# A new order of all engines, another split of the early copies, and a third output tile

## The chip, the cores and the metric

The kernel runs on one core of a Trainium2 chip. The metric is the device time of one execution in microseconds (us), and the time before is the median of three runs. Engines: PE (TensorE, matmuls; PEld is its weight load), DVE (VectorE), ACT (ScalarE), POOL (GpSimd) and SP (SyncE). SP and POOL mostly issue DMAs here.

## What is computed

The inputs are q, k and v of 4 batches, 8 heads, 768 positions and 64 channels, and a feed-forward layer with w_in (512 x 2048), w_out (2048 x 512) and six coefficients. All are float32 in DRAM.

```
scores = q @ k^T / 8, kept where key < 4 or 0 <= query - key < 128
x = softmax(scores) @ v                     -> rows (batch, position), 512 columns
h = x @ w_in
P = a0 + a1 h + a2 h^2 + a3 h^3
Q = 1 + |b0| |h| + |b1| h^2
out = (P / (Q + 1e-6)) @ w_out              -> 3072 x 512, float32
```

## The kernel before, in words

The 3072 output rows are cut into 12 steps of 256 rows, three to a batch. For a step PE makes `scores` (four pieces, one for each pair of heads and half), ACT takes `exps` of them, PE does `attend` (two pieces, scores times V), DVE does `rec` and `norm`, the result is turned (`turn_x`, `placed_x`), and `gemm1` (four pieces of 16 matmuls, one for each quarter of w_in) makes h. ACT copies h to SBUF (`copy_in`) and makes the logarithm and exponential of the reciprocal (`ln`, `exp`); DVE makes the polynomials (`and`, `sqd`, `den`, `even`, `odd`, `odd_h`, `num`, `gate`); PE closes with `gemm2` (four pieces), ACT copies the result out (`copy_out`) and SP stores it. PSUM has four pairs of banks, ps_h, ps_o, ps_m and ps_s, and each piece of PE takes one pair until the copy behind it has freed it.

Each of these is a named piece (`piece`, L1010 and on). The list `ORDER` (L18) gives the number of every piece in the order in which the program issues it, so each engine's queue and each DMA queue runs its pieces in just that order, and an engine that waits for one piece holds all behind it. `ENGINE` says which of ACT and DVE does an early copy, `BANK` which pair of banks a piece takes. A negative number in `ORDER` is a spin of matmuls on constant data (`spin`, L720). No planner runs in the kernel.

Inputs: q and k of step 0 come as float32 on the SP and ACT queues and are cast on chip. All else comes through POOL's one queue and is made bfloat16 on the way: `load_kc`, `load_qc` and `load_vc` (256 KB, Q of step 3 384 KB, Q of step 2 128 KB in SBUF) for K and Q of steps 1 to 3 and V of steps 0 to 2, turned on PE and placed by ACT or DVE; `load_k` and `load_q` (128 KB) for later steps, turned by a DMA transposition of SP; `load_v` (32 or 64 KB a head); `load_w_in` and `load_w_out` (four quarters of 512 KB each). `hold` (L504) is a tiny POOL copy that reads a late element of a result, so that POOL issues nothing behind it until then.

Order of POOL's loads in the opening, before: V0, Q1, K1, V1, Q3, K2, w_in 0, Q2, w_in 1, w_in 3, hold for x of step 0, a head of V3, K3, w_in 2, V2, two heads of V, K5b, K4b, two heads of V, Q tiles 9 and 10, ... The second spin stands in PE's queue ahead of `turn_vs` 1.

Of the kernel before, what the change touches and what calls it, by code (L numbers as in the profile page):

```python
# [65 lines left out]
def kernel(  # L66
# [54 lines left out]
    ENGINE = {('cast_q0', 1): 'DVE',  # L121
               ('place_kc', 3, None): 'DVE',
               ('place_qc', 0, 0): 'ACT',
               ('place_qc', 0, 1): 'ACT',
               ('k_sink', 0): 'DVE',
# [29 lines left out]
             ('attend', 1, 0): 'ps_h',
             ('attend', 1, 1): 'ps_s',
             ('attend', 2, 0): 'ps_m',
             ('attend', 2, 1): 'ps_h',
             ('attend', 3, 0): 'ps_h',
             ('attend', 3, 1): 'ps_m',  # L160
# [21 lines left out]
             ('gemm1', 1, 1): 'ps_o',
             ('gemm1', 1, 2): 'ps_o',
             ('gemm1', 1, 3): 'ps_m',
             ('gemm1', 2, 0): 'ps_m',
             ('gemm1', 2, 1): 'ps_o',
             ('gemm1', 2, 2): 'ps_m',
             ('gemm1', 2, 3): 'ps_o',
# [7 lines left out]
             ('gemm1', 4, 3): 'ps_o',
             ('gemm1', 5, 0): 'ps_s',
             ('gemm1', 5, 1): 'ps_m',
             ('gemm1', 5, 2): 'ps_o',
             ('gemm1', 5, 3): 'ps_h',  # L200
             ('gemm1', 6, 0): 'ps_m',
             ('gemm1', 6, 1): 'ps_o',
# [1227 lines left out]
```

## Time and profile before

| what | value |
|---|---|
| median of three runs | 232.0 us (231.14 to 232.74) |
| the profiled execution | 232.42 us, span 230.7 us |
| PE busy | 215.9 us (94%) |
| DVE busy | 211.1 us (91%) |
| ACT busy | 207.0 us (90%) |
| POOL busy | 97.3 us (42%) |
| moved by DMA | 26.98 MB, mean 117 GB/s; POOL's queue 65024 packets |

The span runs from the first to the last instruction; the 1.7 us between it and the time lie around it. Busy time counts each engine by itself, so three engines of over 90% leave little room: an engine's idle time is worth something only if the other two can use it too. PE's busy time has the spins in it.

### The profile page before, as it was taken

The page shows a single profiled execution, that of the slowest core. Times are in us where ns is not written, and L with a number is a line of the kernel's source. Part 1 is how long each engine was busy: PE and PEld are TensorE (multiplying, and loading weights), DVE is VectorE, ACT ScalarE, POOL GpSimd, SP SyncE. Part 2 cuts the span into 40 slices and gives each one's busy share as a digit, 9 for nine tenths or more (in the row PEclk, how much of TensorE's full clock was granted, in tenths as well). Part 3 has the DMA queues.
Part 4 walks back from the last instruction along what each step waited for, and adds up shares of the span by engine and source line. Part 5 has one row for each costly group of instructions (what it writes and reads, how often), then busy time and mean ns, then how long its engine had stood idle before and what let it go on. Part 6 is the DMA issues. An engine that isn't in the chain of part 4 may idle for free.

```text
span 230.7 us, 7350 instructions
## 1 busy us (share of the span) xinstructions
PE 215.9 (94%) x3249; PEld 147.0 (64%) x3271; DVE 211.1 (91%) x251; ACT 207.0 (90%) x177; POOL 97.3 (42%) x126
## 2 busy tenths in 40 slices
PE   8768999989999999999999999999999999999992
PEld 2546777778747667667677577758856875544441
DVE  3595699879999999999999999999999999999991
ACT  2757889989997999999999999999999999799961
POOL 8914756967559499988199800000000000000000
PEclk9999999999999999999999999999999999999999
DMA  6999999999999999999969998230050200400152
GB/s 182 199 191 199 197 144 103 135 117 121 205 176 141 130 106 150 172 122 124 196 155 133 109 148 162 47 71 0 3 139 3 48 0 0 182 4 0 49 224 91
DMA packets 95237, 26.98 MB, mean 117 GB/s; under 512 B 85862, under 2 KB 92262, under 8 KB 95206
## 3 DMA queue, kind: packets, MB, share of 16 engines
q0 software_dynamic: 65024, 12.98, 90.4%
q1 hardware_dynamic: 28942, 12.75, 29.8%
q10 hardware_dynamic: 1240, 0.79, 1.1%
q8 instruction: 25, 0.41, 0.8%
q14 instruction: 6, 0.05, 0.1%
HBM read 27.30 MB, written 6.29 MB: 146 GB/s over the span
## 4 chain that ended last, share of the span: by engine, by line
PE 69%; DMA 19%; POOL 3%; DVE 3%; issue 2%; ACT 2%; SPq 0%; DVEq 0%; ACTq 0%
PE ps_s L974 13%; PE ps_h L974 11%; PE ps_o L910 9%; PE ps_m L974 9%; PE ps_m L910 7%; DMA w_out_sb<-in_moe_w_out_dram 6%; PE ps_s L910 5%; PE ps_h L910 5%; DMA stage_v<-in_v_dram 4%; DMA k_bf<-in_k_dram 3%; DMA stage_a<-in_k_dram 2%; POOL v L465 2%; DMA ab_row<-in_moe_a_dram 2%; PE ps_o L846 2%; DMA q_bf<-in_q_dram 1%
## 5 line engine op out<-in xcount | busy, mean ns | idle before, releaser
L910 PEld LDWEIGHTS <-w_in_sb 128*128 128x128 bf16 x768 | 73.8, 98 | 13.0 <-issue 1.2
L974 PEld LDWEIGHTS <-g 128*128 128x128 bf16 x386 | 36.4, 98 | 41.6 <-issue 1.4
L954 ACT ACTIVATE lnq<-den 128x4096 f32<-128x4096 bf16 (+3 forms) x18 | 44.6, 2482 | 1.5 <-DVE den L935 1.4
L959 ACT ACTIVATE den<-lnq 128x4096 bf16<-128x4096 f32 (+3 forms) x18 | 44.5, 2484 | 0.2
L465 POOL DMA_DIRECT2D v<-in_v_dram x48 | 35.0, 746 | 3.6 <-DMA w_out_sb<-in_moe_w_out_dram 1.5
L910 PE MATMUL ps_o<-xblk,w_in_sb 128*128 128x256 bf16 x304 | 36.3, 273 | 0.0
L974 PE MATMUL ps_s<-w_out_sb,g 128*128 128x512 bf16 x136 | 32.3, 379 | 0.8 <-issue 0.5
L974 PE MATMUL ps_h<-w_out_sb,g 128*128 128x512 bf16 x121 | 28.6, 379 | 0.9 <-issue 0.5
L964 DVE TENSOR_TENSOR g<-num,den 128x4096 bf16<-128x4096 bf16 (+3 forms) x18 | 28.3, 1572 | 0.3
L935 DVE TENSOR_TENSOR den<-den,sq 128x4096 bf16<-128x4096 bf16 (+3 forms) x18 | 28.3, 1570 | 0.2
L951 DVE TENSOR_TENSOR num<-num,sq 128x4096 bf16<-128x4096 bf16 (+3 forms) x18 | 28.3, 1572 | 0.1
L948 DVE TENSOR_TENSOR sq<-sq,hb 128x4096 bf16<-128x4096 bf16 (+3 forms) x18 | 28.2, 1569 | 0.1
L910 PE MATMUL ps_m<-xblk,w_in_sb 128*128 128x256 bf16 x208 | 24.9, 273 | 0.5 <-DMA w_in_sb<-in_moe_w_in_dram 0.5
L974 PE MATMUL ps_m<-w_out_sb,g 128*128 128x512 bf16 x90 | 21.6, 379 | 0.6 <-issue 0.5
L917 ACT ACTIVATE hb<-ps_o 128x1024 bf16<-128x1024 f32 x19 | 19.5, 1029 | 2.1 <-PE ps_o L910 1.9
L924 ACT ACTIVATE sq<-hb 128x1024 bf16<-128x1024 bf16 (+3 forms) x15 | 20.0, 1341 | 0.1
L427 POOL DMA_DIRECT2D q_bf<-in_q_dram x15 | 16.7, 1111 | 6.0 <-DMA w_out_sb<-in_moe_w_out_dram 2.6
L910 PE MATMUL ps_s<-xblk,w_in_sb 128*128 128x256 bf16 x160 | 19.1, 273 | 0.0
L940 DVE TENSOR_SCALAR num<-sq,acoef 128x4096 bf16<-128x4096 bf16 (+3 forms) x18 | 18.3, 1023 | 0.3
L944 DVE TENSOR_SCALAR sq<-sq,acoef 128x4096 bf16<-128x4096 bf16 (+3 forms) x18 | 18.4, 1021 | 0.3
L507 POOL COPY seen<-x_n 1x1 bf16<-1x1 bf16 x8 | 9.7, 1225 | 17.4 <-DVE x_n L860 17.4
L926 DVE TENSOR_TENSOR sq<-hb 128x2048 bf16<-128x2048 bf16 (+2 forms) x13 | 16.8, 1295 | 0.1
(154 smaller groups left out, 321.5 us busy)
## 6 DMA issues: line engine op xcount, KB each, us to landing
out_dram<-o_t SPq DMA_DIRECT2D x11, 512.0 KB, 3.6
w_in_sb<-in_moe_w_in_dram POOLq DMA_DIRECT2D x4, 512.0 KB, 10.8
k_bf<-in_k_dram POOLq DMA_DIRECT2D x16, 128.0 KB, 6.6
w_out_sb<-in_moe_w_out_dram POOLq DMA_DIRECT2D x4, 512.0 KB, 11.7
q_bf<-in_q_dram POOLq DMA_DIRECT2D x15, 128.0 KB, 5.4
v<-in_v_dram POOLq DMA_DIRECT2D x24, 64.0 KB, 6.3
stage_v<-in_v_dram POOLq DMA_DIRECT2D x3, 256.0 KB, 9.6
v<-in_v_dram POOLq DMA_DIRECT2D x24, 32.0 KB, 5.7
```

Source lines behind the costliest of these rows:

```text
L465: nc.gpsimd.dma_start(out=v_fix[b % 2][half(r), g * NHF:(g + steps) * NHF, hl, 0:D], in_=v[b, h, g * TS:(g + steps) * TS, :].rearrange("(j ...
L910: nc.tensor.matmul(ps[:, n, :], lhsT=w_in_all[:, c, fc * P:(fc + 1) * P], rhs=xblk[m][:, c, :], start=(c == 0), stop=(c == NDMC - 1))
L917: nc.scalar.activation(out=hb[m][:, j * GW:(j + 1) * GW], in_=ps_h.pop((m, j)).rearrange("p n c -> p (n c)"), func=AF.Copy)
L924: nc.scalar.activation(out=sq[m][:, c], in_=hb[m][:, c], func=AF.Square)
L935: nc.vector.tensor_tensor(out=den[m][:, c], in0=den[m][:, c], in1=sq[m][:, c], op=ALU.add)
L944: nc.vector.tensor_scalar(out=sq[m][:, c], in0=sq[m][:, c], scalar1=a3, scalar2=a1, op0=ALU.mult, op1=ALU.add)
L948: nc.vector.tensor_tensor(out=sq[m][:, c], in0=sq[m][:, c], in1=hb[m][:, c], op=ALU.mult)
L951: nc.vector.tensor_tensor(out=num[m][:, c], in0=num[m][:, c], in1=sq[m][:, c], op=ALU.add)
L954: nc.scalar.activation(out=lnq_fix[:, c], in_=den[m][:, c], func=AF.Ln, scale=qsc_reg, bias=1.000001)
L959: nc.scalar.activation(out=den[m][:, c], in_=lnq_fix[:, c], func=AF.Exp, scale=-1.0)
L964: nc.vector.tensor_tensor(out=g_of[m][:, c], in0=num[m][:, c], in1=den[m][:, c], op=ALU.mult)
L974: nc.tensor.matmul(ps_out[own][:, tt, cols], lhsT=g_of[m][:, co:co + P], rhs=w_out_all[:, fc, cols], start=(fc == 0), stop=(fc == NFFC - 1 ...
```

## The change

`ORDER`, `ENGINE` and `BANK` are replaced as a whole. Nothing is computed otherwise, and each engine keeps its number of pieces but for one spin. What the new lists say, read piece by piece:

- POOL issues V0, Q1, K1, K2, V1, Q3, w_in 0, Q2, w_in 1, w_in 3, K3, w_in 2, Q tile 11, a head of V3, two heads of V4, a head of V3, Q tile 9, K5a, V2, Q tiles 10 and 12, a head of V3, K4a, and seven more heads of V. Then comes a hold for h of step 0, K4b, the hold for x of step 0, K5b, the holds for h and x of step 1, two heads of V4, the hold for x of step 3, three heads of V, and the four quarters of w_out.
- PE begins with a spin of 57 in place of 154 (14 matmuls of 512 columns and one of 128, before 13 and two), and the second spin (211: two of 512 and three of 128) is gone. `turn_vc` 2 stays ahead of the first `gemm1` of step 1. The scores of step 4 come behind three of the four `gemm1` of step 2 (before, ahead of all four). Between the first `gemm2` of step 0 and its second half now stand two pieces of scores and one of attend.
- Early copies move between ACT and DVE as the table below shows. On DVE the sink rows of V of batches 1 to 3 (`spread_vs` 1) come ahead of the first `norm`, before behind it.
- `o_sb` has three output tiles in place of two, and `copy_out` of step m waits for the store of step m - 3. The staging tile of the sink rows moves into the free part of the tile that holds q of step 0.

```
 ORDER = [
-    118, 2, 3, 0, -154, 108, 107, 129, 109, 117, 4, 119, 113, 116, 120, 121, 122, 1, 125, 143,
+    118, 2, 3, -57, 0, 108, 107, 109, 119, 113, 5, 117, 120, 121, 122, 129, 143, 144, 1, 125,
...
-    ENGINE = {('cast_q0', 1): 'DVE',
-               ('place_kc', 3, None): 'DVE',
+    ENGINE = {('cast_q0', 1): 'ACT',
+               ('place_kc', 3, None): 'ACT',
-               ('place_qc', 0, 1): 'ACT',
-               ('k_sink', 0): 'DVE',
+               ('place_qc', 0, 1): 'DVE',
+               ('k_sink', 0): 'ACT',
-               ('placed_x', 0, 0): 'ACT',
-               ('placed_x', 0, 1): 'DVE',
+               ('placed_x', 0, 0): 'DVE',
+               ('placed_x', 0, 1): 'ACT',
-               ('placed_x', 1, 1): 'DVE',
+               ('placed_x', 1, 1): 'ACT',
-               ('placed_x', 2, 1): 'DVE',
+               ('placed_x', 2, 1): 'ACT',
-               ('place_vc', 2): 'ACT',
-               ('cast_k0', 0): 'DVE',
-               ('place_k0', 0): 'DVE',
+               ('place_vc', 2): 'DVE',
+               ('cast_k0', 0): 'ACT',
+               ('place_k0', 0): 'ACT',
-               ('cast_q0', 0): 'ACT',
+               ('cast_q0', 0): 'DVE',
-               ('place_kc', 2, None): 'ACT',
-               ('place_qc', 3, 1): 'ACT',
-               ('k_sink', 1): 'ACT',
+               ('place_kc', 2, None): 'DVE',
+               ('place_qc', 3, 1): 'DVE',
+               ('k_sink', 1): 'DVE',
-               ('k_sink', 3): 'ACT'}
+               ('k_sink', 2): 'DVE',
+               ('k_sink', 3): 'DVE'}
...
-             ('turn_vc', 2): 'ps_s',
+             ('turn_vc', 2): 'ps_h',
...
-    o_sb = ctx.enter_context(tc.tile_pool(name="o_sb", bufs=2))
+    o_sb = ctx.enter_context(tc.tile_pool(name="o_sb", bufs=3))
...
-    stage_s = const_pool.tile([SR, B, D], FP32, name="stage_s")
+    stage_s = stage_b[0:SR, NQ0 * H * D:NQ0 * H * D + B * D].rearrange("p (b d) -> p b d", b=B)
...
-                      ends + [("store", m - 2, 0) if m >= 2 else None],
+                      ends + [("store", m - 3, 0) if m >= 3 else None],
...
-          [("gemm2", LAST, 1, parts(LAST) - 1), ("store", LAST - 2, 0)])
+          [("gemm2", LAST, 1, parts(LAST) - 1), ("store", LAST - 3, 0)])
```

## Rows read from the trace of the kernel before

**Rows 1.** Windows: stretch, length, busy PE, PEld, DVE, ACT, POOL, clock, DMA, GB/s.

```profile
6.70:21.70 15.00, 10.53 (x310) 7.98 (x310) 11.24 (x33) 10.22 (x14) 7.00 (x11) 1.00 1.64 188
21.70:31.00 9.30, 8.32 (x245) 6.82 (x242) 6.08 (x13) 8.37 (x11) 6.80 (x10) 1.00 1.51 193
...
36.40:67.50 31.10, 29.41 (x571) 23.31 (x569) 29.11 (x43) 30.22 (x33) 20.59 (x30) 1.00 2.05 144
...
67.50:192.00 124.50, 122.64 (x1867) 86.48 (x1885) 122.86 (x98) 121.03 (x90) 53.53 (x56) 1.00 1.25 102
```

**Rows 2.** Waits of PE: who waited for whom, us in total, times, longest.

```profile
PE ps_s L761 <- DMA qT<-q_bf: 0.7, 1, 0.7
...
PE ps_h L974 <- DMA w_out_sb<-in_moe_w_out_dram: 0.3, 1, 0.3
```

**Rows 3.** Timeline of POOL: start, length, what was issued, [idle before <-releaser].

```profile
20.52 0.18 POOL L507 COPY seen<-x_n 1x1 bf16<-1x1 bf16 x1 [7.94 <-DVE x_n L860]
...
22.25 0.77 POOL L511 DMA_DIRECT2D w_in_sb<-in_moe_w_in_dram  x1
22.99 0.91 POOL L474 DMA_DIRECT2D stage_v<-in_v_dram  x1
...
26.46 1.84 POOL L458 DMA_DIRECT2D k_bf<-in_k_dram  x2
...
30.74 0.90 POOL L427 DMA_DIRECT2D q_bf<-in_q_dram  x1 [1.19 <-DMA w_in_sb<-in_moe_w_in_dram]
33.33 0.89 POOL L427 DMA_DIRECT2D q_bf<-in_q_dram  x1 [1.68 <-DMA stage_v<-in_v_dram]
```

**Rows 4.** DMA view: what, queue, count, KB of each, us from issue to landing.

```profile
w_in_sb<-in_moe_w_in_dram POOLq DMA_DIRECT2D x2, 512.0 KB, 14.4
...
w_in_sb<-in_moe_w_in_dram POOLq DMA_DIRECT2D x1, 512.0 KB, 8.2
...
stage_v<-in_v_dram POOLq DMA_DIRECT2D x1, 256.0 KB, 9.6
...
k_bf<-in_k_dram POOLq DMA_DIRECT2D x2, 128.0 KB, 7.0
...
q_bf<-in_q_dram POOLq DMA_DIRECT2D x1, 128.0 KB, 5.5
...
kT<-k_bf SPq DMA_TRANSPOSE x16, 4.7
```

**Rows 5.** Timeline of PE: second spin, products of steps 0 and 1.

```profile
16.56 0.77 PE L728 MATMUL ps_o<-warm 128*128 128x512 bf16 x5
...
21.74 1.92 PE L910 MATMUL ps_o<-xblk,w_in_sb 128*128 128x256 bf16 x16
...
30.50 1.92 PE L910 MATMUL ps_m<-xblk,w_in_sb 128*128 128x256 bf16 x16 [0.53 <-DMA w_in_sb<-in_moe_w_in_dram]
...
36.40 1.92 PE L910 MATMUL ps_m<-xblk,w_in_sb 128*128 128x256 bf16 x16
```

**Rows 6.** Timeline of DVE in the opening: V0 placed, sink rows spread, second norm.

```profile
12.13 1.21 DVE L679 CAST v<-ps_o 128x1024 bf16<-128x1024 f32 x1
...
17.67 1.89 DVE L555 TENSOR_TENSOR v_sink<-ps_o,ind 128x512 bf16<-128x512 f32 x3
...
19.70 0.75 DVE L860 SCALAR_TENSOR_TENSOR x_n<-ps_s,ratio,rec 128x512 bf16<-128x512 f32 x1
```

**Rows 7.** Groups of DVE by form: count, busy us, mean ns.

```profile
L679 DVE COPY xblk<-ps_h 128x512 bf16<-128x512 bf16 x3 | 1.2, 416 | 0.7 <-PE ps_h L885 0.7
...
L679 DVE COPY kT<-ps_m 128x512 bf16<-128x512 bf16 x1 | 0.7, 671 | 0.0
...
L679 DVE COPY k_sink<-kT 64x16 bf16<-64x16 bf16 x4 | 0.7, 166 | 0.7 <-ACT kT L677 0.7
```

**Rows 8.** Groups of ACT by form: copy of h, copy of x.

```profile
L917 ACT ACTIVATE hb<-ps_o 128x1024 bf16<-128x1024 f32 x19 | 19.5, 1029 | 2.1 <-PE ps_o L910 1.9 <-issue 0.2
...
L677 ACT ACTIVATE xblk<-ps_o 128x512 bf16<-128x512 bf16 x1 | 0.6, 591 | 0.0
```

More of the change, by code (lines that the diff above doesn't have):

```diff
@@ L148 @@
-               ('place_qc', 3, 1): 'ACT',
-               ('k_sink', 1): 'ACT',
+               ('place_kc', 2, None): 'DVE',
+               ('place_qc', 3, 1): 'DVE',
+               ('k_sink', 1): 'DVE',
                ('placed_x', 3, 0): 'DVE',
                ('k_sink', 2): 'DVE',
-               ('k_sink', 3): 'ACT'}
-    BANK = {('attend', 0, 0): 'ps_s',
+               ('k_sink', 3): 'DVE'}
+    BANK = {('attend', 0, 0): 'ps_m',
              ('attend', 0, 1): 'ps_s',
[L155 to L160, printed above, removed]
+             ('attend', 1, 0): 'ps_m',
+             ('attend', 1, 1): 'ps_m',
+             ('attend', 2, 0): 'ps_o',
+             ('attend', 2, 1): 'ps_m',
+             ('attend', 3, 0): 'ps_s',
+             ('attend', 3, 1): 'ps_o',
@@ L161 @@
              ('attend', 4, 0): 'ps_m',
-             ('attend', 4, 1): 'ps_o',
-             ('attend', 5, 0): 'ps_m',
-             ('attend', 5, 1): 'ps_h',
+             ('attend', 4, 1): 'ps_s',
+             ('attend', 5, 0): 'ps_s',
+             ('attend', 5, 1): 'ps_m',
              ('attend', 6, 0): 'ps_m',
-             ('attend', 6, 1): 'ps_o',
+             ('attend', 6, 1): 'ps_h',
              ('attend', 7, 0): 'ps_s',
-             ('attend', 7, 1): 'ps_o',
-             ('attend', 8, 0): 'ps_s',
@@ L170 @@
-             ('attend', 8, 1): 'ps_h',
+             ('attend', 7, 1): 'ps_s',
+             ('attend', 8, 0): 'ps_m',
+             ('attend', 8, 1): 'ps_s',
              ('attend', 9, 0): 'ps_s',
              ('attend', 9, 1): 'ps_o',
-             ('attend', 10, 0): 'ps_s',
-             ('attend', 10, 1): 'ps_o',
+             ('attend', 10, 0): 'ps_h',
+             ('attend', 10, 1): 'ps_s',
              ('attend', 11, 0): 'ps_o',
-             ('attend', 11, 1): 'ps_s',
-             ('gemm1', 0, 0): 'ps_o',
@@ L178 @@
-             ('gemm1', 0, 1): 'ps_s',
-             ('gemm1', 0, 2): 'ps_m',
-             ('gemm1', 0, 3): 'ps_o',
-             ('gemm1', 1, 0): 'ps_s',
[L182 to L188, printed above, removed]
+             ('attend', 11, 1): 'ps_h',
+             ('gemm1', 0, 0): 'ps_h',
@@ L189 @@
+             ('gemm1', 0, 1): 'ps_o',
+             ('gemm1', 0, 2): 'ps_s',
+             ('gemm1', 0, 3): 'ps_m',
+             ('gemm1', 1, 0): 'ps_s',
+             ('gemm1', 1, 1): 'ps_m',
+             ('gemm1', 1, 2): 'ps_s',
+             ('gemm1', 1, 3): 'ps_o',
+             ('gemm1', 2, 0): 'ps_o',
+             ('gemm1', 2, 1): 'ps_h',
+             ('gemm1', 2, 2): 'ps_o',
+             ('gemm1', 2, 3): 'ps_s',
              ('gemm1', 3, 0): 'ps_o',
              ('gemm1', 3, 1): 'ps_m',
-             ('gemm1', 3, 2): 'ps_s',
+             ('gemm1', 3, 2): 'ps_h',
@@ L192 @@
              ('gemm1', 3, 3): 'ps_s',
-             ('gemm1', 4, 0): 'ps_o',
-             ('gemm1', 4, 1): 'ps_o',
+             ('gemm1', 4, 0): 'ps_s',
+             ('gemm1', 4, 1): 'ps_h',
              ('gemm1', 4, 2): 'ps_m',
[L196 to L202, printed above, removed]
+             ('gemm1', 4, 3): 'ps_h',
@@ L203 @@
+             ('gemm1', 5, 0): 'ps_m',
+             ('gemm1', 5, 1): 'ps_s',
+             ('gemm1', 5, 2): 'ps_m',
+             ('gemm1', 5, 3): 'ps_o',
+             ('gemm1', 6, 0): 'ps_o',
+             ('gemm1', 6, 1): 'ps_m',
              ('gemm1', 6, 2): 'ps_s',
              ('gemm1', 6, 3): 'ps_o',
-             ('gemm1', 7, 0): 'ps_m',
-             ('gemm1', 7, 1): 'ps_m',
+             ('gemm1', 7, 0): 'ps_h',
+             ('gemm1', 7, 1): 'ps_o',
              ('gemm1', 7, 2): 'ps_o',
-             ('gemm1', 7, 3): 'ps_s',
@@ L209 @@
-             ('gemm1', 8, 0): 'ps_s',
+             ('gemm1', 7, 3): 'ps_m',
+             ('gemm1', 8, 0): 'ps_m',
              ('gemm1', 8, 1): 'ps_s',
@@ L231 @@
              ('gemm2', 6, 0, 0): 'ps_m',
-             ('gemm2', 7, 0, 0): 'ps_s',
+             ('gemm2', 7, 0, 0): 'ps_o',
              ('gemm2', 8, 0, 0): 'ps_m',
-             ('gemm2', 9, 0, 0): 'ps_s',
-             ('gemm2', 10, 0, 0): 'ps_h',
-             ('gemm2', 11, 0, 0): 'ps_s',
-             ('gemm2', 11, 1, 0): 'ps_o',
-             ('scores', 0, 0): 'ps_h',
-             ('scores', 0, 1): 'ps_s',
-             ('scores', 0, 2): 'ps_s',
-             ('scores', 0, 3): 'ps_m',
-             ('scores', 1, 0): 'ps_m',
-             ('scores', 1, 1): 'ps_s',
-             ('scores', 1, 2): 'ps_m',
-             ('scores', 1, 3): 'ps_h',
-             ('scores', 2, 0): 'ps_m',
-             ('scores', 2, 1): 'ps_h',
-             ('scores', 2, 2): 'ps_o',
-             ('scores', 2, 3): 'ps_o',
-             ('scores', 3, 0): 'ps_o',
-             ('scores', 3, 1): 'ps_s',
-             ('scores', 3, 2): 'ps_o',
-             ('scores', 3, 3): 'ps_h',
-             ('scores', 4, 0): 'ps_s',
+             ('gemm2', 9, 0, 0): 'ps_h',
+             ('gemm2', 10, 0, 0): 'ps_o',
+             ('gemm2', 11, 0, 0): 'ps_h',
+             ('gemm2', 11, 1, 0): 'ps_s',
+             ('scores', 0, 0): 'ps_m',
+             ('scores', 0, 1): 'ps_m',
+             ('scores', 0, 2): 'ps_h',
+             ('scores', 0, 3): 'ps_s',
+             ('scores', 1, 0): 'ps_m',
+             ('scores', 1, 1): 'ps_h',
+             ('scores', 1, 2): 'ps_h',
+             ('scores', 1, 3): 'ps_s',
+             ('scores', 2, 0): 'ps_h',
+             ('scores', 2, 1): 'ps_o',
+             ('scores', 2, 2): 'ps_s',
+             ('scores', 2, 3): 'ps_h',
+             ('scores', 3, 0): 'ps_s',
+             ('scores', 3, 1): 'ps_m',
+             ('scores', 3, 2): 'ps_h',
+             ('scores', 3, 3): 'ps_o',
+             ('scores', 4, 0): 'ps_m',
              ('scores', 4, 1): 'ps_s',
@@ L259 @@
              ('scores', 5, 1): 'ps_o',
-             ('scores', 5, 2): 'ps_o',
-             ('scores', 5, 3): 'ps_m',
+             ('scores', 5, 2): 'ps_m',
+             ('scores', 5, 3): 'ps_o',
              ('scores', 6, 0): 'ps_m',
              ('scores', 6, 1): 'ps_o',
-             ('scores', 6, 2): 'ps_h',
+             ('scores', 6, 2): 'ps_m',
              ('scores', 6, 3): 'ps_h',
@@ L268 @@
              ('scores', 7, 2): 'ps_m',
-             ('scores', 7, 3): 'ps_h',
-             ('scores', 8, 0): 'ps_s',
-             ('scores', 8, 1): 'ps_h',
-             ('scores', 8, 2): 'ps_m',
+             ('scores', 7, 3): 'ps_o',
+             ('scores', 8, 0): 'ps_m',
+             ('scores', 8, 1): 'ps_o',
+             ('scores', 8, 2): 'ps_o',
              ('scores', 8, 3): 'ps_o',
-             ('scores', 9, 0): 'ps_s',
+             ('scores', 9, 0): 'ps_h',
              ('scores', 9, 1): 'ps_s',
-             ('scores', 9, 2): 'ps_o',
-             ('scores', 9, 3): 'ps_o',
+             ('scores', 9, 2): 'ps_h',
+             ('scores', 9, 3): 'ps_s',
              ('scores', 10, 0): 'ps_s',
              ('scores', 10, 1): 'ps_o',
-             ('scores', 10, 2): 'ps_o',
-             ('scores', 10, 3): 'ps_m',
-             ('scores', 11, 0): 'ps_s',
-             ('scores', 11, 1): 'ps_h',
-             ('scores', 11, 2): 'ps_h',
-             ('scores', 11, 3): 'ps_s',
+             ('scores', 10, 2): 'ps_m',
+             ('scores', 10, 3): 'ps_s',
+             ('scores', 11, 0): 'ps_o',
+             ('scores', 11, 1): 'ps_s',
+             ('scores', 11, 2): 'ps_s',
+             ('scores', 11, 3): 'ps_h',
              ('turn_k0', 0): 'ps_m',
```

42 lines of the change are left out of this document (21 added, 21 removed), and 83 rows, old and new, of the table ORDER.

## The prediction, made before the changed kernel was run

> **What bounds the kernel.** The busy shares of the page, over 90% for PE, DVE and ACT alike, say that no single engine sets the time, so I read the busy time by stretch next. From 67.5 to 192 us PE idles 1.86 us, DVE 1.64 and ACT 3.5 of 124.5 us [rows 1]: nothing of size that an order could win back. What idles lies ahead of that. Between 6.7 us, the end of the warm-up, and 21.7 us, the first product with w_in, PE idles 4.47 us and spins 0.77 us more [rows 1, 5]; from 21.7 to 31.0 us it idles 0.98 us; from 36.4 to 67.5 us PE idles 1.69 us, DVE 1.99 and ACT 0.88 [rows 1]. Two of PE's late waits have a name: 0.7 us for Q of step 4, 0.3 us for w_out [rows 2]. Behind the opening stands one line of POOL's loads, and what the reader is to see there is how late they land: w_in 3, issued at about 11.8 us, lands 14.4 us later at 26.2; w_in 2 at 22.25 + 8.2 = 30.45 us, and PE stands 0.53 us until then; V2 at 22.99 + 9.6 = 32.6 us [rows 3, 4, 5].
>
> **The change, part by part.**
>
> *w_in in a row.* POOL stands 7.94 us at the hold for x of step 0, and w_in 2 comes behind it [rows 3]. That looks like the cause of the 0.53 us, but the line was never dry: between 26.2 and 30.45 us, the landings of w_in 3 and w_in 2, it carried a head of V, K3 and w_in 2, 800 KB in 4.25 us, about 190 GB/s. All that stood ahead of w_in 2 stands ahead of it again, except the head of 32 KB, 0.2 us. So w_in 2 lands at 30.2 us: 0.2 us gained, between 0 and the whole 0.53.
>
> *V2 behind other loads.* POOL keeps eight loads in flight: Q9 waits at 30.74 us for w_in 2, the eighth before it, and Q10 at 33.33 us for V2, the eighth before that [rows 3]. In the new line w_in 2 is the eighth before V2, so V2 is issued at 30.2 us and not at 22.99. The seven between (three of 128 KB, two of 64, two of 32, in all 576 KB) go first. Before, 320 KB of such loads (two heads of V, K5b, K4b) landed between V2 at 32.6 us and K4b at 27.4 + 7.0 = 34.4 us [rows 3, 4], about 180 GB/s; so the seven take 3.2 us and V2 1.4 us more: 34.8 us. A load that meets a short line lands 5.5 us after its issue [rows 4]: 35.7 us. I take the later, 35.7; the upper end is V2's own 9.6 us [rows 4], 39.8 us. PE comes to the turn of V2 at about 35.2 us: two products from 30.2 us of 1.92 us at most [rows 5], three scores and a turn of x, 1.4 us. It stands 0.5 us, and the first product of step 1, at 36.40 us before [rows 5], could start at 36.2. That product also needs a copy of x that now stands on ACT behind the last copy of h of step 0: 34.4 + 0.2 + 1.03 + 0.59 [rows 8] is 36.2 us as well, so the 0.5 us costs nothing more.
>
> The page "DMA: Bandwidth & Descriptors" of the Trainium skill (Specifications) wants pieces of 512 bytes for full rate, and a row of q, k or v in DRAM is 64 float32, 256 bytes. Read as half the rate it would put V2 at 38 us and the time at about 233.3 us. The trace does not agree: 180 GB/s for these rows beside 190 for w_in and K3 with longer ones.
>
> *The opening on DVE and ACT.* By size (1.2 us for 1024 columns, 0.67 for 512, for 768 about 0.95, between the two, 0.42 for x, two of 0.17 for K's columns [rows 6, 7]) DVE gets V2, K2, two Q of 768, an x, a cast and two sets of columns, 6.1 us, and gives K3, two casts, half of K0, three x and one set of columns, 4.6 us: 1.5 us more for it, and somewhat less for ACT. DVE idles 3.8 us before 21.7 us and 3.2 us before 31.0 [rows 1], so by amount it is covered; without that cover it costs 1.5 us. The order costs more: the sink rows of three batches, 1.89 us, stood between the first norm and the second, which ended at 20.45 us [rows 6]; now they precede both. DVE's queue from V0's placing (at 12.25 us, one small mask later than 12.13) gives: sink rows until 17.7, both norms until 19.95, K2 placed at 21.2, which frees the banks for the next scores, last copy of x at 21.6 us. PE then has 1.0 us of scores to do, and its first product starts at 22.25 us, 0.5 us later than at 21.74 [rows 5]; one piece of scores of step 1, 0.4 us, is already behind it. Net 0.1 us lost. Since some twenty small waits decide, I bound it by 1.5 us either way, a third of the 4.47 us.
>
> *K1 and K2 first.* V1 and Q3 land later by one load of 256 KB, 1.4 us. PE did not wait for them before, and it comes to Q3 only when the sink rows are done, at 17.7 us: 0, or up to 0.5 us if that cover fails.
>
> *The spins.* The first is one matmul of 512 columns longer and one of 128 shorter, and five of such take 0.77 us [rows 5]: at most 0.1 us, while q has to be cast anyway. The second, 0.77 us, goes; PE waits for DVE in its place: 0.
>
> *Steps 1 to 4.* The scores of step 4, which stood 0.7 us for Q [rows 2], come behind three groups of products of step 2, over 5 us. Their loads come later too: K4b is the eleventh issue after V2, at 0.65 to 0.9 us each [rows 3] some 39 us, lands at 45, and two transpositions on SP behind it, the last with 4.7 us to landing [rows 4], end at 51 us, against PE at 53. The 0.3 us for w_out goes likewise, as 1.4 us of scores and attend now stand ahead. PE could win 1.0 us, DVE 1.99, ACT only its 0.88 [rows 1]. I take 0.8, between 0 and 1.7.
>
> *Third output tile, shared staging tile.* No copy of the output waits for a store in PE's, DVE's or ACT's rows, so the wait that goes was free; stores of SP that come later behind transpositions have three tiles of cover. 0.
>
> *After 67.5 us.* The same pieces in another order on engines 97 to 99% busy: 0, between -0.5 and +2.5 us (2% of 124.5).
>
> **The sum** is made against the profiled execution's 232.42 us. The start of step 1 carries the opening, w_in and V2: -0.2. Steps 1 to 4: -0.8. That is 231.4 us; the median of the runs stands 0.4 us under the profiled one, which would make it 231.0. I forecast 231.2 us.
>
> **The rivals.**
>
> *V2 late, slower.* Past 35.9 us PE stands at V2's turn with all else behind it, and nothing later can take it up: 231.2 + (landing - 35.9). Slower than before from 36.7 us on, by over 1% from 39.0; 39.8 us gives 235.1. For it: the issue moves 7 us later, and the page's rule above. Against: the rate above [rows 3, 4].
>
> *No gain.* DVE has 1.5 us more to do and hardly rests from 24 us on; its 1.99 us of idle time up to 67.5 [rows 1] pays for the copies, not for PE's waits: 232.2 us.
>
> *A looser late stretch.* New banks and orders cost 1 to 2% of 124.5 us: 233 to 235 us. No row speaks for or against.
>
> *A tighter opening.* K2 lands two loads earlier, and over half of PE's 4.47 us goes: 228.5 us. Against: DVE's queue as walked.
>
> *The clock falls.* PE's granted clock reads 1.00 in every stretch, the 2.4 GHz level, though it idles 30% of 6.7 to 21.7 us [rows 1]; the second spin stood in that stretch. At 1.2 GHz for half of the 8.3 us of PE work that follow [rows 1], 4 us are lost, some of it covered: 234.5 us. The page "TensorE: Matmul & The Clock Gate" of the Trainium skill (HAM oscillation) has PE fall to half rate after long idling; no run here shows such a fall.
>
> **How the numbers follow.** Forecast 0.40, no gain 0.16, V2 late 0.13, looser late stretch 0.10, tighter opening 0.17, clock 0.04. About 1%, 2.3 us, is what a measurement of this kernel tells from no change. Under 229.7 us: most of the tighter opening and a fifth of the forecast, 0.24. Over 234.3 us: the later half of V2, half of the loose stretch, the clock and the ends of the unknown terms, 0.20. Between: 0.56. The range takes in the tighter opening and V2 up to 39 us: 228.5 to 234.6.
>
> **What would show it.** PE's first product at 22.2 us; w_in 2 landing at 30.2 and V2 at 35.7; the first product of step 1 at 36.2; no wait of PE for qT or w_out after that; 2 us of idle PE from 67 to 192. The forecast falls if PE waits over 1 us for V2, if DVE never rests from 24 to 60 us while PE waits for it, or if the late stretch has over 3 us of idle PE.

## The result, and the profile after

The changed kernel takes 233.64 us in the median of 19 runs (233.0 to 237.45), the kernel before 232.0 us (231.14 to 233.22) in 19 runs on the same chip: a ratio of 1.0079, 95% interval [1.0059, 1.0100]. It is slower by 1.8 us where the forecast was 0.8 us faster; the range 228.5 to 234.6 us held it. The profiled execution took 235.26 us, with a span of 233.6 us. That is 1.6 us above the median, so the rows below show more loss than the 1.8 us of the ratio.

The line numbers of the changed kernel are one lower. Its windows first, the same four stretches as in [rows 1] and then three short ones (columns as there):

```profile
6.70:21.70 15.00, 11.38 (x303) 8.71 (x305) 12.44 (x36) 10.10 (x16) 9.87 (x13) 0.89 1.63 188
21.70:31.00 9.30, 8.54 (x246) 7.04 (x239) 6.82 (x18) 8.79 (x11) 3.20 (x5) 1.00 1.62 188
36.40:67.50 31.10, 28.66 (x568) 22.93 (x567) 26.79 (x39) 27.42 (x29) 19.84 (x28) 0.95 1.23 132
67.50:192.00 124.50, 122.84 (x1844) 83.88 (x1859) 122.94 (x101) 120.83 (x90) 47.94 (x58) 1.00 1.17 109
15.00:20.00 5.00, 4.34 (x140) 3.46 (x140) 3.83 (x11) 2.77 (x4) 1.52 (x2) 0.66 1.53 198
40.00:45.00 5.00, 2.88 (x83) 2.15 (x81) 3.13 (x7) 3.43 (x5) 4.32 (x9) 0.87 1.26 105
45.00:50.00 5.00, 5.00 (x57) 3.76 (x54) 3.39 (x7) 3.07 (x5) 0.00 (x0) 0.79 1.62 159
```

From 36.4 to 67.5 us PE, DVE and ACT all rest more than in [rows 1], DVE 4.31 us where it was 1.99, and most of that lies between 40 and 50 us. The waits of PE and DVE name it (columns as in [rows 2]); the waits for qT and w_out of [rows 2] are gone:

```profile
DVE x_n L859 <- POOL seen L506: 2.1, 1, 2.1
PE ps_h L884 <- DVE x_n L859: 2.1, 1, 2.1
...
PE ps_s L909 <- DMA w_in_sb<-in_moe_w_in_dram: 0.8, 1, 0.8
```

DVE waits for POOL. This is the timeline of POOL (columns as in [rows 3]):

```profile
30.60 0.88 POOL L473 DMA_DIRECT2D stage_v<-in_v_dram  x1 [1.97 <-DMA w_in_sb<-in_moe_w_in_dram]
...
35.36 3.99 POOL L464 DMA_DIRECT2D v<-in_v_dram  x6
39.60 0.62 POOL L464 DMA_DIRECT2D v<-in_v_dram  x1 [0.24 <-DMA v<-in_v_dram]
40.22 0.18 POOL L506 COPY seen<-hb 1x1 bf16<-1x1 bf16 x1
40.77 0.90 POOL L457 DMA_DIRECT2D k_bf<-in_k_dram  x1 [0.37 <-DMA k_bf<-in_k_dram]
41.66 0.18 POOL L506 COPY seen<-x_n 1x1 bf16<-1x1 bf16 x1
```

The last row is the hold for x of step 0. It stood at 20.52 us in [rows 3], where POOL waited 7.94 us for the x; now the x has been ready since 19 us, and POOL comes to the hold only at 41.66 us, since V2, two Q tiles, two K, eight heads of V and another hold stand ahead of it. And x has two buffers: the `norm` of step 2 writes into that of step 0, so it may not run before the hold has read it. DVE's timeline shows what waited for that (columns as in [rows 6]):

```profile
41.87 0.75 DVE L859 SCALAR_TENSOR_TENSOR x_n<-ps_m,ratio,rec 128x512 bf16<-128x512 f32 x1 [2.12 <-POOL seen L506]
```

And PE's shows what waited for DVE, with the products that answer to [rows 5] ahead of it:

```profile
22.21 1.92 PE L909 MATMUL ps_h<-xblk,w_in_sb 128*128 128x256 bf16 x16
...
30.36 1.92 PE L909 MATMUL ps_s<-xblk,w_in_sb 128*128 128x256 bf16 x16 [0.76 <-DMA w_in_sb<-in_moe_w_in_dram]
...
36.14 1.91 PE L909 MATMUL ps_o<-xblk,w_in_sb 128*128 128x256 bf16 x16 [0.16 <-ACT xblk L676]
...
42.68 0.40 PE L884 MATMUL ps_h<-ident,x_n 128*128 128x128 bf16 x4 [2.12 <-DVE x_n L859]
...
44.02 3.41 PE L909 MATMUL ps_s<-xblk,w_in_sb 128*128 128x256 bf16 x16
```

Up to 36 us the opening goes as walked (against [rows 5]: the first product 0.47 us later, that of step 1 0.26 us earlier). V2's row in the DMA view answers to [rows 4]:

```profile
stage_v<-in_v_dram POOLq DMA_DIRECT2D x1, 256.0 KB, 4.7
```

In the opening DVE spreads the sink rows first and ends the second norm at 18.9 us (20.45 in [rows 6]); then it waits 1.10 us for PE before it places K2:

```profile
15.16 1.88 DVE L554 TENSOR_TENSOR v_sink<-ps_o,ind 128x512 bf16<-128x512 f32 x3
...
18.19 0.74 DVE L859 SCALAR_TENSOR_TENSOR x_n<-ps_s,ratio,rec 128x512 bf16<-128x512 f32 x1
...
20.04 1.23 DVE L678 COPY kT<-ps_m 128x1024 bf16<-128x1024 bf16 x1 [1.10 <-PE ps_m L660]
```

The copies last as priced from [rows 7, 8]; a Q of 768 on DVE and an x on ACT, in the groups by form:

```profile
L678 DVE COPY qT<-ps_o 128x768 bf16<-128x768 bf16 x2 | 1.9, 956 | 0.0
```

```profile
L676 ACT ACTIVATE xblk<-ps_o 128x512 bf16<-128x512 bf16 x2 | 1.2, 594 | 0.9 <-PE ps_o L879 0.9
```

Then, past 40 us, PE stands 2.12 us, and the product behind takes 3.41 us instead of 1.92, at a mean granted clock of 0.87 and 0.79: part of that time (0.50 from 44 to 47 us) at 1.2 in place of 2.4 GHz. PE's first output product starts at 65.2 us, before at 63.4, and PE ends at 229.5, before at 226.7 us. So the first theory was: the late hold costs 2.1 us, and the clock behind it 1.5 us more.

### The profile page after: what moved, and what is told of

The parts are those of the page before. It is cut to its first block, busy times and chain, and to the rows that moved or that the text cites. A ratio compares the mean times of both kernels' runs of the same rounds, so it can differ in the third digit from the quotient of the medians.

```text
span 233.6 us, 7355 instructions
## 1 busy us (share of the span) xinstructions
PE 219.2 (94%) x3246; PEld 147.4 (63%) x3266; DVE 213.1 (91%) x252; ACT 206.5 (88%) x176; POOL 91.2 (39%) x126
## 5 line engine op out<-in xcount | busy, mean ns | idle before, releaser
L464 POOL DMA_DIRECT2D v<-in_v_dram x48 | 34.3, 739 | 5.3 <-DMA w_in_sb<-in_moe_w_in_dram 3.5
L973 PE MATMUL ps_h<-w_out_sb,g 128*128 128x512 bf16 x136 | 32.5, 379 | 0.7 <-issue 0.3
L909 PE MATMUL ps_s<-xblk,w_in_sb 128*128 128x256 bf16 x208 | 26.4, 283 | 1.0 <-DMA w_in_sb<-in_moe_w_in_dram 0.8
L909 PE MATMUL ps_o<-xblk,w_in_sb 128*128 128x256 bf16 x192 | 23.0, 273 | 0.2 <-ACT xblk L676 0.2
L973 PE MATMUL ps_o<-w_out_sb,g 128*128 128x512 bf16 x92 | 21.5, 379 | 0.4 <-issue 0.2
L909 PE MATMUL ps_h<-xblk,w_in_sb 128*128 128x256 bf16 x160 | 19.1, 273 | 0.0
L426 POOL DMA_DIRECT2D q_bf<-in_q_dram x15 | 15.8, 1059 | 5.2 <-DMA w_in_sb<-in_moe_w_in_dram 1.9
L916 ACT ACTIVATE hb<-ps_s 128x1024 bf16<-128x1024 f32 x13 | 13.3, 1025 | 3.4 <-PE ps_s L909 3.3
```

Of the source, the lines that this page charges most:

```text
L464: nc.gpsimd.dma_start(out=v_fix[b % 2][half(r), g * NHF:(g + steps) * NHF, hl, 0:D], in_=v[b, h, g * TS:(g + steps) * TS, :].rearrange("(j ...
L909: nc.tensor.matmul(ps[:, n, :], lhsT=w_in_all[:, c, fc * P:(fc + 1) * P], rhs=xblk[m][:, c, :], start=(c == 0), stop=(c == NDMC - 1))
L973: nc.tensor.matmul(ps_out[own][:, tt, cols], lhsT=g_of[m][:, co:co + P], rhs=w_out_all[:, fc, cols], start=(fc == 0), stop=(fc == NFFC - 1 ...
```

## The experiments

Each ratio is to the kernel before, run on the same chip in the same rounds. Edits of `ORDER` are told by the pieces' names.

**The hold, put back early** (`hold_early`) or **spins in the opening** (`spins`, 211 ahead of `scores` 0 1 and 107 ahead of `attend` 0 1), and **both** (`hold_spins`):

```diff
 # POOL's entries of ORDER
+hold x 0
 load_vc 2
 ...
 hold h 0, load_k 4 1
-hold x 0
```

> The changed kernel with one entry of the order moved: POOL's wait (hold) for x of step 0 stands right before the load of the fourth pair's V instead of behind the loads that follow it. Theory 1 (that hold, read at 41.66 us in the changed kernel, keeps DVE's norm of step 2 waiting 2.1 us and PE with it): DVE's norm of step 2, second half, starts at about 39.8 instead of 41.87, PE's longest wait (2.1 for x_n) is gone, the granted clock stays at 1.00 in 40 to 50, the first product of that stretch takes 1.9 instead of 3.4 us, and the time falls by 2 to 3.5 us, to 230.2 to 231.7. Theory 2 (the clock falls by itself, whatever DVE does): the wait is gone but the clock still falls after 42, and the time falls by 0 to 1 only. Rival (DVE's extra 2 us of work, or the late order, sets the time): the wait is gone and its time comes back before 67 us or in the late stretch; the time stays at 233 or above.

> The changed kernel with two idle-time spins of PE put in (0.77 us and 0.4 us by the rows of the kernel before) ahead of the second scores and the second attention product of step 0; the hold for x of step 0 stays late. Theory 1: PE's wait of 2.1 us at 42 us stays, and the clock falls behind it; the time stays within 1 us of the changed kernel's 233.6. Theory 2 for the opening: the clock stays at 1.00 in 15 to 20 us and the first product starts 0.3 to 0.5 us earlier, at about 21.8; worth at most 0.5 in the total. Rival (clock of the opening costs nothing or the spins delay the products): the first product starts at 22.2 or later.

> The changed kernel with both edits: the hold for x of step 0 early and the two spins. Theory 1 and 2 together: no wait of 2.1 us, clock 1.00 from 15 to 60, first product at about 21.8, time 229.8 to 231.4, that is, faster than both kernels. Rival (DVE's work or the late order sets the time): 233 or above.

Measured: 1.0010 [0.9988, 1.0033], 1.0084 [1.0049, 1.0119] and 1.0065 [1.0035, 1.0094]. The hold alone gives back 0.7% against the changed kernel's 1.0079 (taken in other rounds), 1.6 us, and no norm waits for POOL; the norm runs at 40.87 us, and the product behind it takes 1.92 us again, as the timelines of `hold_early` show, DVE's and then PE's:

```profile
40.87 0.74 DVE L860 SCALAR_TENSOR_TENSOR x_n<-ps_m,ratio,rec 128x512 bf16<-128x512 f32 x1
...
78.42 0.34 DVE L679 COPY k_sink<-kT 64x16 bf16<-64x16 bf16 x2 [1.14 <-DMA kT<-k_bf]
```

The product that took 3.41 us:

```profile
42.89 1.92 PE L910 MATMUL ps_s<-xblk,w_in_sb 128*128 128x256 bf16 x16
```

But 2.1 + 1.5 us were in sight, and the forecast of 230.2 to 231.7 us was missed: the second row of DVE is a new wait, 1.14 us for the transposition of K, in a place where DVE comes at 79.13 us in the changed kernel and doesn't wait. With hold and spins it is 3.21 us, and of the 1.6 us only 0.4 are left (1.0084 with the spins alone, 1.0065 with both), less than the intervals.

The spins alone did not do what they were put in for: the clock reads 0.81 from 15 to 20 us, and the first product starts at 23.12 us. Their profile also has a shorter wait for the hold, 1.01 us, and behind it a clock of 1.00 from 40 to 50 us; the time is that of the changed kernel all the same.

**The hold made late in the kernel before** (`before_hold_late`):

```diff
 # POOL's entries of ORDER (kernel before)
-hold x 0     # ahead of w_in 2
 ...
+hold h 1, load_v 3 4, load_v 3 3, load_v 3 1, hold x 0     # now ahead of norm 2 1
```

> The kernel before with only this done: POOL's hold for x of step 0 goes behind the hold for h of step 1 and three loads of V of step 3, as the changed kernel has it behind loads. Theory 1: POOL passes it at about 42.1 us, DVE's norm of step 2 (second half), at 40.17 before, waits about 2 us for it, PE's waits for x_n grow by 1 to 2 us, and the time rises by 1 to 3.5 us, to 233 to 235.5 (the upper end if the clock falls behind the wait). Rival (a norm that is 2 us late is hidden by other work of DVE and PE): within 0.5 us of 232.0.

Measured: 0.9998 [0.9975, 1.0021]. The wait was there, shorter than meant; DVE's timeline:

```profile
43.67 0.75 DVE L860 SCALAR_TENSOR_TENSOR x_n<-ps_h,ratio,rec 128x512 bf16<-128x512 f32 x1 [1.30 <-POOL seen L507]
```

It took the place of other rests: DVE rested 1.66 us in all from 36 to 58 us, 1.96 in the kernel before. The opening of this execution was late as well (clock 0.66 from 15 to 20 us, first product at 23.66 us, before at 21.74), so that the norm came due at 42.4 us and not at 40.17. So a late hold cost nothing that can be told in the old opening; this run doesn't say what a wait of 2.1 us would have cost.

**Opening and late order apart** (`open_new_late_old`, `open_old_late_new`, and `hold_late_old`: the first with the hold early). Each takes one kernel's `ORDER`, `ENGINE` and `BANK` up to the first `gemm2`, and the other's order and banks for the pieces that are left:

```diff
-ORDER = new
+ORDER = new[:first gemm2] + [n for n in old if n not in new[:first gemm2]]
```

> The changed kernel up to its first output product (at 65 us), with the split of evictions and the banks that belong to it; from there the entries that are left stand in the order, and with the banks, of the kernel before. Theory A (all of the loss is made ahead of the first output product, by the late hold and what follows it): first output product at about 65, end as in the changed kernel, 1.006 to 1.010 of the kernel before. Theory B (the new order of the late stretch costs 1 to 2 us of its own): 1.000 to 1.004. Theory C (DVE has about 2 us more work in the new opening, and the late stretch, in which DVE rests 1 per cent, can't take it in): as theory A, with DVE busy about 213.

> The kernel before up to its first output product (63.4 us), and from there the new order and banks, with three output tiles. Theory A and theory C: within 0.3 per cent of the kernel before. Theory B: 1 to 2 us longer, 1.004 to 1.009. If the new late order is a gain that the opening hides: 0.3 to 1 us shorter.

> As the first of these, with the hold for x of step 0 ahead of the load of the fourth pair's V. Theory A: 1.6 us less than the first, about the time of the kernel before (0.998 to 1.002). Theory B: shorter than the kernel before, 0.992 to 0.997, since the opening's wait is gone and the old late order has what the new one lost. Theory C: 1.000 to 1.005, with DVE busy 213 to 214.

Measured: 1.0048 [1.0014, 1.0081], 1.0046 [1.0019, 1.0073] and 0.9983 [0.9951, 1.0016]. None of the three theories alone gives this: the new opening costs 1.1 us and the new late order another 1.1, and together they are the change's 1.8. The opening's loss goes with the hold: without the late hold the new opening is 0.4 us shorter than the old, within what can be told from nothing, and 1.5 us shorter than with it (the two intervals just touch). The wait is there in `open_new_late_old`, whose PE shows it, and a slow product with it:

```profile
43.00 0.55 PE L885 MATMUL ps_h<-ident,x_n 128*128 128x128 bf16 x4 [2.26 <-DVE x_n L860]
45.05 2.62 PE L910 MATMUL ps_s<-xblk,w_in_sb 128*128 128x256 bf16 x16
```

**DVE's extra work** (`hold_vc2_act`):

```diff
-('place_vc', 2): 'DVE',     # hold_early
+('place_vc', 2): 'ACT',
```

> The changed kernel with the hold for x of step 0 early, and the eviction of the fourth pair's V (1.21 us on DVE) given back to ACT, as in the kernel before. Theory C (DVE's work sets the time from 36 us on): 0.8 to 1.3 us less than with the hold alone, 0.995 to 0.998 of the kernel before, DVE busy about 212.8. Theory A or B (DVE's work is not it): within 0.3 us of the kernel with the hold alone, or longer by up to 1 us if ACT, which evicts the products there, is the bound.

Measured: 1.0078 [1.0047, 1.0108], 0.7% more than with the hold alone (1.0010). ACT, which copies h there, brings V2 late, and PE's first attend of step 1 waits 1.52 us for it, where it waited 0.69 us for DVE in `hold_early`:

```profile
39.94 0.38 PE L846 MATMUL ps_m<-v,e 64*64 64x65 bf16 x24 [1.52 <-ACT v L677]
```

So the copy stands better on DVE; but as the edit made a wait of its own, it doesn't tell what DVE's extra work costs. `hold_late_old` says more on that: it has the whole new split (DVE busy 212.9 us, 211.1 in the kernel before) and its 0.9983 lies under theory C's 1.000 to 1.005, though the interval reaches into it.

**w_out earlier, and the tiles alone** (`hold_early_wout`, `hold_spins_wout`, `hold_late_old_wout`, `before_tiles`):

```diff
 # POOL's entries of ORDER
+load_w_out 0, load_w_out 1, load_w_out 2, load_w_out 3
 hold x 3
```

```diff
-o_sb = ctx.enter_context(tc.tile_pool(name="o_sb", bufs=2))
+o_sb = ctx.enter_context(tc.tile_pool(name="o_sb", bufs=3))
 # and the waits for store m - 3, and stage_s in stage_b, as in the change
```

> The changed kernel with the hold for x of step 0 early, and the four loads of w_out ahead of the hold for x of step 3, for which POOL waited 4.1 us (43.5 to 49.7 us with the hold alone). Theory D (in the new late order the transposition of the third batch's K comes behind w_out's bytes: DVE's k_sink waited 1.14 us for it at 78.4 us, and in the run with spins 3.21 us, so that a gain of the opening is given back): the loads of w_out are issued about 5 us earlier, DVE doesn't wait for K's transposition, DVE's idle time from 67.5 to 100 us falls from 1.62 to about 0.4, and the time is 0.8 to 1.4 us less than with the hold alone: 0.995 to 0.998 of the kernel before. Rival (the late stretch is set by the DVE's own work and order, whatever K does): as with the hold alone, 1.000 to 1.003.

> As the last, with the two spins of the opening as well. Theory D: the 3.21 us for which DVE's k_sink waited in the run with hold and spins are gone; 2 to 3.5 us less than there (1.0065), 0.991 to 0.998. Rival: within 1 us of it, 1.002 to 1.008.

> The kernel with the new opening, the early hold for x of step 0 and the old late order (0.9983 of the kernel before), with the four loads of w_out ahead of the hold for x of step 3 (POOL waited 4.8 us for that hold, and 2.9 and 1.7 us behind w_out's landings). Theory D says that in the old late order nothing waits for K's transposition: the time stays within 0.4 us, 0.996 to 1.000. If the loads behind w_out are late for something else there (DVE's idle time of 0.71 us from 67.5 to 100): 0.5 us less.

> The kernel before with three output tiles alone (a tile is awaited three steps after its store instead of two, and the sinks' staging lies in the queries' staging to make room). All theories: 0.998 to 1.002, since the late stretch of the kernel before doesn't wait for a store. If the tiles were to blame for the new late order's 1.1 us: 1.004 or more.

Measured: 1.0422 [1.0355, 1.0489], 1.0453 [1.0385, 1.0521], 1.0379 [1.0314, 1.0444], and 0.9981 [0.9951, 1.0010]. The tiles cost nothing that can be told. w_out issued about 7 us sooner (from 44.71 us on in `hold_spins_wout`, from 51.74 in `hold_spins`) costs 9 to 10 us: its 2 MB go ahead of the Q, K and V of the next steps. PE's timeline of `hold_spins_wout`:

```profile
60.80 0.30 PE L761 MATMUL ps_m<-qT,k_sink 128*32 128x128 bf16 x4 [6.30 <-DMA qT<-q_bf]
66.34 0.36 PE L772 MATMUL ps_h<-qT,kT 64*64 64x192 bf16 x8 [0.97 <-DMA kT<-k_bf]
68.64 0.63 PE L846 MATMUL ps_m<-v,e 64*64 64x65 bf16 x12 [1.15 <-DMA v<-in_v_dram]
```

The edit made what it was to cure worse, so it says nothing on theory D.

**Only the waiting instruction moved** (`hold_ksink`, `hold_spins_ksink`: k_sink behind three DVE pieces; `open_old_late_new_rec`: the reciprocal behind the shift), and `hold_late_old` with the spins:

```diff
 # DVE's entries of ORDER
-k_sink 2
 placed_x 4 1, odd_h 2 0, and 3 0
+k_sink 2
 rec 5 0
```

```diff
 # DVE's entries of ORDER
-rec 4 1
 and 2 0
+rec 4 1
 norm 4 1
```

> The changed kernel with the hold for x of step 0 early, and with DVE's two copies of the third batch's sink keys (k_sink) moved behind the next four entries of DVE's order, so that the eviction of x, a product of 2.29 us and a shift of 1.22 us run first. Theory D (DVE rests there for the transposition of K): the wait of 1.1 us at 78 us is gone, DVE's idle time from 67.5 to 100 us falls from 1.62 to 0.5, and the time is about 1 us less than with the hold alone (1.001): 0.995 to 0.998. Theory E (the time of the late stretch is set elsewhere and the wait would only move): 0.999 to 1.003.

> The same with the two spins of the opening. Theory D: the wait of 3.2 us for K's transposition is gone; 2 to 3 us less than with hold and spins (1.0065): 0.994 to 0.998. Theory E: 1.003 to 1.008.

> The old opening with the new late order (1.0046), and in DVE's order the reciprocal of step 4, for which DVE rested 1.03 us at 68.75 us, behind the shift of 1.18 us that came after it. Theory D in its general form (the new late order has DVE wait for things that a later opening would have had ready): the rest is gone, DVE's idle time from 67.5 to 100 us falls from 1.46 to about 0.5, and the time falls by about 1 us to 0.998 to 1.002. Theory E: 1.003 to 1.007.

> The new opening with the early hold, the old late order, and the two spins. If the granted clock of 0.66 from 15 to 20 us costs what its matmuls show there (0.4 us on the first product) and the spins keep it up: 0.2 to 0.5 us less than without spins (0.9983), 0.994 to 0.998, which is faster than both kernels. If the clock of the opening is hidden by the waits for loads, or the spins delay as much as they save: 0.997 to 1.002.

Measured: 1.0017 [0.9985, 1.0049], 0.9996 [0.9971, 1.0021], 1.0045 [1.0016, 1.0073], 1.0015 [0.9984, 1.0045]. Where the wait for K was 3.21 us, its removal gave 0.7% back (1.0065 to 0.9996), which is theory D, though the bound of 0.998 was missed; where it was 1.14 us, the time did not move (1.0010 and 1.0017). And in `open_old_late_new_rec` the rest did not go. DVE's timeline of `open_old_late_new` has the 1.03 us:

```profile
68.75 0.21 DVE L854 RECIPROCAL rec<-ps_s 128x8 f32<-128x8 f32 x1 [1.03 <-PE ps_s L846]
```

And that of `open_old_late_new_rec` what stood in its place:

```profile
72.13 2.29 DVE L964 TENSOR_TENSOR g<-num,den 128x4096 bf16<-128x4096 bf16 x1 [0.75 <-ACT den L959]
77.70 0.35 DVE L679 COPY k_sink<-kT 64x16 bf16<-64x16 bf16 x2 [0.52 <-DMA kT<-k_bf]
```

1.03 us had become 0.75 + 0.52: DVE comes sooner to the next waits, for ACT and for K. The spins bring nothing to `hold_late_old`.

**The clock by itself, and the late order in two** (`spin_wait`, `old_to_gate8`):

```diff
 # PE's entries of ORDER (changed kernel)
 gemm1 1 2
+-132     # eight matmuls of 512 columns into ps_h
 turn_x 2 1
```

> The changed kernel with the hold for x of step 0 still late, and PE doing eight idle matmuls of 512 columns (about 1.9 us) just where it waits 2.12 us for x of step 2. It takes nothing off the path; it only keeps PE at work. If the granted clock falls after 42 us because PE rested there (0.87 and 0.79 of full from 40 to 50 us; the product behind took 3.41 instead of 1.92 us): the clock stays at 1.00, that product takes 1.92 us, and the time falls by 0.7 to 1.6 us, to 1.001 to 1.005 of the kernel before. If the clock's loss is hidden behind DVE or ACT, or the fall is not PE's rest: within 0.4 us of the changed kernel, 1.006 to 1.010.

> The kernel before up to DVE's ninth gate (136.9 us in the kernel before), and the new order and banks from there, with three output tiles. If the new late order loses its 1.1 us (old opening with all of the new late order: 1.0046) by what DVE rests between 63 and 137 us: 0.998 to 1.002. If it loses them in its last part, where DVE needs 26.9 us from the end of its 13th gate to that of its 18th, and 24.6 us in the kernel before: 1.003 to 1.007.

Measured: 1.0094 [1.0061, 1.0126] and 1.0157 [1.0118, 1.0196]. The spin did what it should. PE's timeline of `spin_wait`:

```profile
41.81 1.89 PE L728 MATMUL ps_h<-warm 128*128 128x512 bf16 x8
43.92 0.40 PE L885 MATMUL ps_h<-ident,x_n 128*128 128x128 bf16 x4 [0.22 <-DVE x_n L860]
...
45.18 1.92 PE L910 MATMUL ps_s<-xblk,w_in_sb 128*128 128x256 bf16 x16
```

Its windows (columns as in [rows 1]):

```profile
40.00:45.00 5.00, 4.78 (x107) 3.26 (x95) 3.05 (x8) 2.58 (x4) 3.08 (x7) 1.00 1.03 73
45.00:50.00 5.00, 5.00 (x112) 4.11 (x102) 4.97 (x10) 4.62 (x6) 0.93 (x2) 1.00 1.71 137
```

The clock stays at 1.00, the product takes 1.92 us, and the time is no shorter than the changed kernel's. So the clock's fall follows PE's rest. That it costs nothing does not follow, for this execution lost time in two other places. POOL stood 1.92 us for a load of K and came to the hold at 42.90 us, 1.24 us later than in the changed kernel, and DVE waited for the hold and later for the transposition of K. POOL's timeline and then DVE's:

```profile
42.01 0.90 POOL L458 DMA_DIRECT2D k_bf<-in_k_dram  x1 [1.92 <-DMA k_bf<-in_k_dram]
42.90 0.18 POOL L507 COPY seen<-x_n 1x1 bf16<-1x1 bf16 x1
```

```profile
43.11 0.75 DVE L860 SCALAR_TENSOR_TENSOR x_n<-ps_m,ratio,rec 128x512 bf16<-128x512 f32 x1 [1.95 <-POOL seen L507]
...
80.31 0.35 DVE L679 COPY k_sink<-kT 64x16 bf16<-64x16 bf16 x2 [1.28 <-DMA kT<-k_bf]
```

PE's first output product, in the changed kernel and in `spin_wait`:

```profile
65.19 1.89 PE L973 MATMUL ps_h<-w_out_sb,g 128*128 128x512 bf16 x7
```

```profile
65.00 1.89 PE L974 MATMUL ps_h<-w_out_sb,g 128*128 128x512 bf16 x8
```

From the turn of x behind the wait to this product PE needs 22.5 us in the changed kernel (42.68 to 65.19) and 22.4 in `open_new_late_old`, the two with the fall, and 21.1 in `spin_wait` (43.92 to 65.00) and 20.9 in `spins`, the two without. So in these executions the fall cost about 1.4 us up to there. Whether the median of the changed kernel's runs has that loss is open: `spins`, without the fall in its profile, is at 1.0084. `old_to_gate8` settles nothing, since the seam made a wait of its own (PE 2.29 us for ACT's e at 138 us).

## Why the prediction was wrong

*w_in in a row, V2.* Right: w_in 2 let PE go at 30.36 us (30.2 forecast), V2 was issued at 30.60 (30.2) and landed at 35.3 us (35.7). The half rate for the seven loads ahead of V2 that I read out of "DMA: Bandwidth & Descriptors" (Specifications) in the Trainium skill, which would have brought V2 at 38 us, did not show.

*The opening on DVE and ACT, K1 and K2, the spins.* Right in size: first product at 22.21 us for 22.25, first of step 1 at 36.14 for 36.2. The 22.21 is partly luck. DVE ended the norms at 18.93 us and not at 19.95, and then waited 1.10 us for PE, which worked at a granted clock of 0.66; with 1.00 there, the same entries bring the first product at 21.70 us (`hold_early`) and 21.59 (`spin_wait`). The clock of 0.66 from 15 to 20 us is not the missing second spin's doing. The same window of `open_old_late_new`, which has the old opening with both its spins, and of `spin_wait`, which has the new one without, read:

```profile
15.00:20.00 5.00, 4.24 (x99) 2.87 (x103) 3.28 (x13) 2.76 (x4) 0.00 (x0) 0.66 1.57 193
```

```profile
15.00:20.00 5.00, 3.66 (x152) 2.88 (x152) 4.77 (x11) 2.68 (x4) 1.32 (x2) 1.00 1.52 195
```

*Steps 1 to 4: the step that failed.* I gave this term -0.8 us, and the two waits that it counted did go. What I left out is a move that the change itself told of: the hold for x of step 0 went down POOL's queue, behind V2 and some dozen loads. I walked V2 through POOL's eight loads in flight, and K4b to 39 us, and did not walk the hold, which comes right after K4b. K4b is the twelfth load behind V2 and not the eleventh, so the same count gives some 40 us for it and about 41 for the hold; the trace has 40.77 and 41.66 us. Nor did I ask who waits for it, the norm of step 2, due at about 39.8 us. By the runs the late hold costs 1.5 us (1.0048 to 0.9983) to 1.6 us (1.0079 to 1.0010) with the new opening; with the spins in both it is 0.4 us (1.0084 to 1.0065), as the wait for K takes the rest. Without the late hold the new opening gains 0.4 us (0.9983), between 1.1 us gained and 0.4 lost: the -0.8 is not shown, and not excluded.

*After 67.5 us.* Taken as 0, with bounds of -0.5 and +2.5. The new late order costs 1.1 us with the old opening (1.0046), and by differences about 0.7 with the new one (1.0079 - 1.0048, 1.0010 - 0.9983): the rival "looser late stretch", at half of its size. My sign for it, over 3 us of idle PE, could not have shown it: PE rests 1.66 us from 67.5 to 192 us, before 1.86. The traces do show it. From the first output product to the end of the span four executions with the old late order take 166.8 to 167.7 us (kernel before, `before_hold_late`, `open_new_late_old`, `hold_late_old`; 169.1 in `before_tiles`, whose PE stood 1.4 us for w_out). Six with the new one take 168.3 to 168.4 us, with either opening (changed kernel, `open_old_late_new`, `open_old_late_new_rec`, `spins`, `hold_ksink`, `hold_spins_ksink`), and those in which DVE stood over 1 us for K take 169.3 us and more. The chain of waits differs too: PE's products nearly throughout from 67.5 us on in the kernel before, DVE's work from 145 us to its last gate in the changed one. A few rows of the latter (start, length, what):

```profile
144.78 0.75 DVE x_n L859
145.53 2.21 DVE sq L947
147.74 0.02 issue
147.76 2.30 DVE num L950
```

So: the hold 1.5, the late order 0.7, less 0.4 for the rest of the opening, makes 1.8 us. The three are steps of one chain of kernels (before, `hold_late_old`, `open_new_late_old`, changed), so the sum has to come out and does not test them. None of the three signs under which the forecast was to fall showed, though it fell: PE did not wait for V2, DVE rested, and the late stretch has 1.66 us of idle PE.

*Third output tile.* Right: 0.9981.

*The rivals.* "No gain" for DVE's work does not account for the loss: `hold_late_old` has that work and is no slower than the kernel before. "The clock falls" came true in part. In the opening the clock read 0.66 from 15 to 20 us, and the 0.5 us that it cost the first product were taken up by 36 us; behind the wait of 2.12 us it read 0.87 and 0.79, and cost about 1.4 us up to the first output product of that execution. "TensorE: Matmul & The Clock Gate" (HAM oscillation) of the Trainium skill has PE start slow after it has stood for data. The two traces in which it stood 2.12 and 2.26 us agree.

*Open.* What in the late order makes the 0.7 to 1.1 us. DVE rests 1.5 us from 67.5 to 100 us in `open_old_late_new` and 0.5 in the kernel before, but with one rest removed others took its place. From the end of DVE's 13th gate to that of its 18th it is 26.9 us in every profile with the new late order and 24.6 in every one with the old; up to the 13th gate the new order is about 1.3 us shorter (136.3 us from the first output product in the changed kernel, 137.6 before). That order of the last gates was not tested apart. Open is also what the clock's fall costs in the median run, and why the late hold costs nothing in the old opening. No version here is faster than the kernel before by more than its interval; the best, `hold_late_old`, is at 0.9983 [0.9951, 1.0016].

## What to carry to other kernels

When loads are moved, list every instruction that stays behind them on the same queue, the tiny ones first, and ask for each who waits for it and through which buffer: a 0.18 us copy that frees a buffer cost 1.5 us here, the moved loads nothing that can be told. Test a reorder in parts that can be swapped (opening of one, rest of the other) before a cause is believed. And when three engines are 97 to 99% busy, a wait taken away in one place may bring the next wait, as the one for K here. A profile is one execution: this one lay 1.6 us above the median, and not all that it showed is in the ratio.

## What the runs showed of the hardware

A fall of the granted clock came behind PE's longer rests: after 2.12 us in the changed kernel (0.50 from 44 to 47 us) and after 2.26 us in `open_new_late_old` (0.81 and 0.85 from 40 to 45 and 45 to 50 us). With the rest filled by 1.9 us of idle matmuls it stayed at 1.00, as it did behind rests of 1.01 us in `spins` and 1.22 us in `before_hold_late`.

The clock of one order is not the same in every execution, and a loss of clock can be taken up. With the new opening's entries ahead of it, 15 to 20 us read 0.66 in the changed kernel, `hold_late_old` and `open_new_late_old`, and 1.00 in `hold_early` and `spin_wait`. The first product came at 22.1 to 22.2 us in the first three and at 21.6 to 21.7 in the other two, the first product of step 1 at 36.1 to 36.5 us in all five.

And four loads of w_out, 2 MB, issued 7 us sooner, made a loss of 9 to 10 us out of a gain that was put at 1 us.
